# Moving two input tiles to the crossbar, five weight slices to a second DMA queue, and a gate vector to five rows, at the head of a TensorE-bound kernel

## The chip, the cores and the metric

One core of one Trainium2 chip. The metric is the device time of one execution in microseconds (us); each kernel is run several times and the median is given.

## The reference

Linear attention (A) and a token-mixing MLP (B) over the same 2048 x 640 input, mixed by a sigmoid gate. Cut to what matters here:

```python
x = A_x                                           # [1, 2048, 640] bf16
g = sigmoid((x * gate_w).sum(-1, keepdims=True))  # gate_w: [640]
qkv = x @ wqkv                                    # q, k, v; 32 heads of 20
pq, pk = phi(q), phi(k)
num = pq @ einsum(pk, v);  den = pq . sum(pk)     # linear attention
a = (num / den) @ wo
b = x1 + gelu(ln(x1) @ w3) @ w4                   # x1 = x + mix(gelu(ln(x) @ w1)) @ w2
out = g * a + (1 - g) * b
```

## The kernel before

TensorE needs x transposed (`xT`) as its stationary operand, the one that is loaded as weights. The 16 tiles of 128 tokens get it in two ways: tiles 0 to 3 are turned on TensorE (five 128 x 128 transposes a tile, then a copy out of PSUM, the memory that TensorE writes), tiles 4 to 15 by the crossbar, a transposing DMA from `x_tok` to `xT`. `wq` and `wk` (here `wkg`, with columns for the row sum and the gate) come in five slices of 160 KB, one for each 128 rows of the contraction. All big loads go through SyncE's queue, in this order:

```python
sch.dma("act", junk[:, 0, 0:32]..., "touch")               # a few bytes of wqkv, ScalarE's queue
dma_in(x_tok[:, 0:2, :], ..., "x01")                       # tiles 0 and 1, 320 KB
dma_in(x_tok[:, 2:4, :], ..., "x23")
for k in range(KD):                                        # KD = 5
    load_wq(k)
for k in range(KD):
    dma_in(wkg[:, k, 0:D], A_wqkv[128 * k:128 * (k + 1), D:2 * D], "wk%d" % k)
dma_in(wkg[:, :, D + 2:D + 3], gate_w.rearrange("(k p o) -> p k o", p=128, o=1), "gw", noncontig=True)
for c in range(1, NCH):                                    # tiles 4 to 15, four at a time
    dma_in(x_tok[:, 4 * c:4 * c + 4, :], ..., "xc%d" % c)  # 640 KB
    for t in range(4 * c, 4 * c + 4):
        sch.dma("sp", xT[:, :, 128 * t:128 * (t + 1)], x_tok[:, t, :], ..., transpose=True)
```

The head of TensorE's program. `stream` takes several tiles through one weight slice before it goes to the next, so a slice is needed later; each (tile, slice) is a pair of matmuls, 512 and 128 columns wide:

```python
addA(("warm",), 0.0, lambda: warmup(NWARM, 427.0))         # NWARM = 5
for i in range(4):
    addA(("tx", i), 0.28, lambda i=i: t_x(i))              # turn tile i on TensorE
    if i % 2:
        addA(("warm", i), 0.0, lambda: warmup(NWARM2, 300.0))  # NWARM2 = 2
addA(("q", 3), 5.44, q_four)                               # q of tiles 0..3, slice by slice
addA(("k", 0), 1.36, k_first)
for i in range(1, 4):
    addA(("k", i), 1.36, lambda t=i: k_tile(t))
for i in range(4, NT + 2):
    ...                                                    # q and k of tile i, and so on
```

Waits are derived from the tiles that each operation reads and writes. (The rest of the kernel, which the change does not touch, is cut.)

Of the kernel before, what the change touches and what calls it, by code (L numbers as in the profile page):

```python
# [5 lines left out]
BF16 = mybir.dt.bfloat16  # L6
F32 = mybir.dt.float32
ACTF = mybir.ActivationFunctionType
# [3 lines left out]
D = 640  # L12
# [3 lines left out]
NT = S // 128  # L16
# [408 lines left out]
def _build(nc, A_x, A_wqkv, A_wo, B_w1, B_w2, B_w3, B_w4, gate_w, out, dbg=None, stop=None):  # L425
# [45 lines left out]
    def psb(b, n0, n1):  # L471
        return ps[:, b, :].bitcast(BF16)[:, n0:n1]

    ones_c = pa.alloc("ones_c", [128, 768], BF16)
    ident = pa.alloc("ident", [128, 128], BF16)
    mask = pa.alloc("mask120", [128, 6, 20], BF16)
    mask_t = pa.alloc("mask_t", [128, 6, 20], BF16)
    negh = pa.alloc("negh", [128, 4], F32)
    st1 = pa.alloc("st1", [128, 8, NT], F32)
# [57 lines left out]
    def pair():  # L537
        best = None
        for k_ in range(4):
            q_ = (bank_rr[0] // 2 + k_) % 4  # L540
            tf = 0.0
            ok = True
            for b in (2 * q_, 2 * q_ + 1):
                if b in bank_pend or b in bank_hold:
                    ok = False
                lk = sch.locks.get(b)
                if lk is not None:
                    tf = max(tf, sch.ev_time.get((lk[1].sem, lk[1].val), 1e18))
            if ok and (best is None or tf < best[0]):
                best = (tf, 2 * q_)  # L550
        b = best[1]
        bank_rr[0] = b + 2
        bank_pend.update((b, b + 1))
        return b
# [94 lines left out]
    def activation(out_ap, in_ap, func, scale=1.0, bias=0.0, accum=None):  # L649
        rd = [in_ap] + [a for a in (scale, bias) if not isinstance(a, (int, float))]  # L650
        wr = [out_ap] + ([accum] if accum is not None else [])
        n = nfree(out_ap)
        cost = max(150.0, 100.0 + 0.833 * n + (70.0 if in_psum(in_ap) else 0.0)) + 45.0 * (len(rd) - 1)
        if accum is not None:
            cost += 91.0
        st_ = ACT_SET.get(func)
        if st_ is not None and st_ != sch.act_func:
            cost += 1290.0
            sch.act_func = st_
        if accum is not None:  # L660
            return act(lambda e: e.activation(out_ap, in_ap, func, bias=bias, scale=scale, accum_out=accum), rd, wr, cost=cost)  # L661
        return act(lambda e: e.activation(out_ap, in_ap, func, bias=bias, scale=scale), rd, wr, cost=cost)  # L662

    def memset(engf, ap, val):
        return engf(lambda e: e.memset(ap, val), [], [ap])  # L665

    def copy(engf, out_ap, in_ap):
        cost = None
        if engf is dve and in_ap.dtype == BF16 and out_ap.dtype == BF16:
            cost = 65.0 + nfree(out_ap) / 1.92  # L670
        return engf(lambda e: e.tensor_copy(out_ap, in_ap), [in_ap], [out_ap], cost=cost)
# [7 lines left out]
    def dma_in(out_ap, in_ap, key, **kw):  # L679
        return sch.dma("sp", out_ap, in_ap, key, **kw)  # L680

    sch.dma("act", junk[:, 0, 0:32].rearrange("p (k f) -> p k f", k=2),
            A_wqkv.rearrange("(k p) f -> p k f", p=128)[:, 0:KD:KD - 1, 0:16], "touch")
    dma_in(x_tok[:, 0:2, :], x2[0:256, :].rearrange("(n p) d -> p n d", p=128), "x01")
    def load_wq(k):
        dma_in(wq[:, k, :], A_wqkv[128 * k:128 * (k + 1), 0:D], "wq%d" % k)

    dma_in(x_tok[:, 2:4, :], x2[256:512, :].rearrange("(n p) d -> p n d", p=128), "x23")
    for k in range(KD):
        load_wq(k)  # L690
    for k in range(KD):
        dma_in(wkg[:, k, 0:D], A_wqkv[128 * k:128 * (k + 1), D:2 * D], "wk%d" % k)
    dma_in(wkg[:, :, D + 2:D + 3], gate_w.rearrange("(k p o) -> p k o", p=128, o=1), "gw", noncontig=True)
    for c in range(1, NCH):
        dma_in(x_tok[:, 4 * c:4 * c + 4, :], x2[512 * c:512 * (c + 1), :].rearrange("(n p) d -> p n d", p=128), "xc%d" % c)
        for t in range(4 * c, 4 * c + 4):
            sch.dma("sp", xT[:, :, 128 * t:128 * (t + 1)], x_tok[:, t, :], "trx%d" % (t % 4), transpose=True)

    k_done = {}

# [18 lines left out]
            n = min(R6, D - R6 * r)  # L719
            sch.dma("pool", wo_aug[0:n, r, :], A_wo[R6 * r:R6 * r + n, :], "wo", group_total=6, deps=dp)  # L720

    memset(pool, ones_c[:], 1.0)
    aselect(ident[:], ones_c[:, 0:128], [[-1, 128]], ALU.is_equal, 0, 1)
    memset(pool, wkg[:, :, D:D + 2], 1.0)
    memset(pool, negh[:], -0.5)
# [14 lines left out]

    IT = _Items()
    NWARM = 5
    NWARM2 = 2

    def t_x(t):
        b = bank()
        tr_group(b, [x_tok[:, t, 128 * k:128 * (k + 1)] for k in range(KD)])
        src = psb(b, 0, D).rearrange("p (k c) -> p k c", k=KD)
        dst = xT[:, :, 128 * t:128 * (t + 1)]
        if t % 2:  # L750
            activation(dst, src, ACTF.Copy)
        else:
            copy(dve, dst, src)

    def phi(b, dst, after_exp=None):
        se = slot("E", 3)
        src = psf[:, 512 * b:512 * b + D]
        activation(Er[:, se, :], src, ACTF.Exp)
        if after_exp is not None:
            after_exp()  # L760
        ts(dve, Er[:, se, :], Er[:, se, :], 1.0, EPS_PHI, ALU.min, ALU.add)
        return stt(dst, src, 1.0 + EPS_PHI, Er[:, se, :], ALU.add, ALU.max)

    def k_tile(t):
        tok = slice(128 * t, 128 * (t + 1))
        b = pair()
        mm_group(ps[:, b, 0:512], [(xT[:, k, tok], wkg[:, k, 0:512]) for k in range(KD)])
        mm_group(ps[:, b + 1, 0:131], [(xT[:, k, tok], wkg[:, k, 512:D + 3]) for k in range(KD)])
        k_out(t, b)
# [57 lines left out]
    def warmup(n, cyc):  # L827
        b = bank()

        def fn(e):  # L830
            ins = None
            for _ in range(n):
                ins = e.matmul(ps[:, b, :], ones_c[:, 0:128], ones_c[:, 128:640], start=True, stop=True)  # L833
            return ins
        pe(fn, [ones_c[:, 0:640]], [ps[:, b, :]], cost=n * cyc)
# [5 lines left out]
        mm_group(ps[:, b + 1, 0:128], [(xT[:, k, tok], wq[:, k, 512:D]) for k in range(KD)])  # L841
        phi(b, pq_tok[:, t, :])

    def stream(tiles, w, n2, land, done):
        nxt = {t: 0 for t in tiles}
        bs = {t: pair() for t in tiles}
        now = 0.0
        while nxt:
            t = next((t for t in tiles if t in nxt and nxt[t] * land <= now), min(nxt, key=lambda t: nxt[t]))
            now = max(now, nxt[t] * land) + 0.272  # L850
            k, b = nxt[t], bs[t]
            l = xT[:, k, 128 * t:128 * (t + 1)]

            def fn(e, l=l, b=b, k=k):
                e.matmul(ps[:, b, 0:512], l, w[:, k, 0:512], start=(k == 0), stop=(k == KD - 1))  # L855
                return e.matmul(ps[:, b + 1, 0:n2], l, w[:, k, 512:512 + n2], start=(k == 0), stop=(k == KD - 1))  # L856
            pe(fn, [w[:, k, 0:512 + n2], l], [ps[:, b, 0:512], ps[:, b + 1, 0:n2]], cost=272.0)
            nxt[t] += 1
            if nxt[t] == KD:
                del nxt[t]  # L860
                done(t, b)

    def q_four():
        stream(range(4), wq, 128, 0.5, lambda t, b: phi(b, pq_tok[:, t, :]))

    def k_out(t, b):
        k_done[t] = phi(b, pk_tok[:, t, :], lambda: activation(lr[:, t, :], ps[:, b + 1, 129:131], ACTF.Copy))
        activation(junk[:, 0, :], x_tok[:, t, :], ACTF.Square, accum=st1[:, 1, t:t + 1])

    def k_first():  # L870
        stream(range(1), wkg, 131, 0.0, k_out)

    def addA(name, dur, fn, deps=()):
        IT.add("A", name, dur, fn, deps)

    addA(("warm",), 0.0, lambda: warmup(NWARM, 427.0))
    for i in range(4):
        addA(("tx", i), 0.28, lambda i=i: t_x(i))
        if i % 2:
            addA(("warm", i), 0.0, lambda: warmup(NWARM2, 300.0))  # L880
    addA(("q", 3), 5.44, q_four)
    addA(("k", 0), 1.36, k_first)
    for i in range(1, 4):
        addA(("k", i), 1.36, lambda t=i: k_tile(t))
    for i in range(4, NT + 2):
        if i < NT:
            addA(("q", i), 1.36, lambda t=i: q_tile(t))
            addA(("k", i), 1.36, lambda t=i: k_tile(t))
        for t in range(3) if i == 4 else (i - 2,):
            addA(("g0", t), 0.27, lambda t=t: gt_step(0, t, t + 1), deps=[(("k", t), 2.0)])  # L890

    IT.add("LW", ("lw1",), 0.0, load_w1, deps=[(("k", 5), 0.0)])
    IT.add("LW", ("lw2",), 0.0, load_w2, deps=[(("k", 8), 0.0)])
# [276 lines left out]
            IT.add("W3", ("w3", c, j), 1.08, lambda c=c, j=j: w3_group(c, j), deps)  # L1170
        IT.add("W3", ("w3h", c), 0.76, lambda c=c: w3_half(c))
    for t in range(NT):
        deps = [(("zb",), 1.0), (("q", max(t, 3)), 2.0)]
        if t < 7:
            i = (5 * t) // 2 + 3
            deps.append((("w1", i // KD, i % KD), 0.0))
        else:
            i = 2 * (t - 7)
            deps.append((("w3", i // KFF, i % KFF), 0.0))
        IT.add("QN", ("qs", t), 0.0, lambda t=t: qn_sum(t), deps)  # L1180
        IT.add("QN", ("qn", t), 0.0, lambda t=t: qn_scale(t), [(("qs", t), 0.0)])
        IT.add("QT", ("qt", t), 0.0, lambda t=t: qt_tile(t), deps=[(("qn", t), 3.2), (("w2", NT - 1), 0.5), (("t2", NT - 1), 0.0)])
# [60 lines left out]
```

## Time and profile before

| | before |
|---|---|
| median of 3 runs known at first | 266.19 us |
| span of the profiled run | 264.6 us |
| TensorE (PE) busy | 260.2 us, 98% |
| first q matmul | 6.71 us |
| first wk matmul (the first 20 pairs are done) | 12.14 us |

The page's first line, its line of busy times, and the first line of its part on the chain of work that ended last:

```profile
span 264.6 us, 4340 instructions
PE 260.2 (98%) x1729; PEld 136.7 (52%) x1729; DVE 145.8 (55%) x242; ACT 107.9 (41%) x218; POOL 91.4 (35%) x148
...
PE 98%; DVE 0%; POOL 0%; issue 0%; POOLq 0%
```

TensorE is the whole chain. A microsecond that TensorE idles is a microsecond of the result. The list of TensorE's waits (who waited for what, total us, times, longest) has one line, at the start:

```profile
PE ps L833 <- POOL ones_c L665: 1.6, 1, 1.6
```

The head, from the timeline of TensorE (start, duration, engine, line, operation, out<-in, count). A busy time overlaps the next one a little, as matmuls are pipelined; read the starts.

```profile
1.59 2.32 PE L833 MATMUL ps<-ones_c 128*128 128x512 bf16 x5 [1.59 <-POOL ones_c L665]
3.91 1.25 PE L617 MATMUL ps<-ident,x_tok 128*128 128x128 bf16 x10
4.95 0.94 PE L833 MATMUL ps<-ones_c 128*128 128x512 bf16 x2
5.72 0.72 PE L617 MATMUL ps<-ident,x_tok 128*128 128x128 bf16 x10
6.28 0.60 PE L833 MATMUL ps<-ones_c 128*128 128x512 bf16 x2
6.71 0.38 PE L855 MATMUL ps<-wq,xT 128*128 128x512 bf16 x1
```

SyncE's queue over the same stretch (start and duration of the issue, not of the transfer):

```profile
1.81 2.36 SPq L283 DMA_DIRECT2D wq<-in_A_wqkv_dram  x5
4.21 2.33 SPq L283 DMA_DIRECT2D wkg<-in_A_wqkv_dram  x5
6.58 0.43 SPq L282 DMA_DIRECT2D wkg<-in_gate_w_dram  x1
7.06 0.54 SPq L283 DMA_DIRECT2D x_tok<-in_A_x_dram  x1
12.94 6.17 SPq L279 DMA_TRANSPOSE xT<-x_tok  x4
```

And the view of the tile `wkg`, its line on the time from issue to landing (the largest is that of gate_w):

```profile
DMA to landing us min/median/max: 3.6/3.7/4.8
```

### The profile page before, as it was taken

How to read it: one execution, taken by the hardware profiler on the slowest of the kernel's cores; microseconds unless marked ns; L12 is line 12 of the kernel's file. 1: busy time of each engine (PE TensorE's matmuls, PEld its weight loads, DVE VectorE, ACT ScalarE, POOL GpSimd, SP SyncE). 2: the span in 40 equal slices, each digit the busy share in tenths (PEclk: the TensorE clock that was granted, in tenths of full speed). 3: DMA queues.
4: the chain of work that ended last, by engine and by line, in shares of the span. 5: the costliest groups of instructions: out<-in, count | busy, mean ns of one | idle time of the engine just before them, and what ended most of it. 6: DMA issues, size and time to landing. Idle time of an engine off the chain costs nothing.

```text
span 264.6 us, 4340 instructions
## 1 busy us (share of the span) xinstructions
PE 260.2 (98%) x1729; PEld 136.7 (52%) x1729; DVE 145.8 (55%) x242; ACT 107.9 (41%) x218; POOL 91.4 (35%) x148
## 2 busy tenths in 40 slices
PE   7999999999999999999999999999999999999995
PEld 4555555555555555554445445545454455445553
DVE  1486877899713797999776986321212121122242
ACT  3496677741365757766651211212321322121000
POOL 4003995759764025688730204000120011021020
PEclk9999999999999999999999999999999999999999
DMA  7765998634567897255456831120000200002011
GB/s 229 218 100 133 199 182 136 191 85 22 102 122 106 252 379 137 39 99 49 92 113 126 111 63 25 42 85 2 0 0 11 90 0 0 2 0 102 0 50 50
DMA packets 50627, 24.78 MB, mean 94 GB/s; under 512 B 42028, under 2 KB 49197, under 8 KB 50608
## 3 DMA queue, kind: packets, MB, share of 16 engines
q1 hardware_dynamic: 49184, 21.23, 37.0%
q0 software_dynamic: 1152, 3.28, 5.4%
q8 instruction: 13, 0.21, 0.4%
q14 instruction: 6, 0.05, 0.1%
q10 hardware_dynamic: 272, 0.01, 0.1%
HBM read 12.05 MB, written 2.62 MB: 55 GB/s over the span
## 4 chain that ended last, share of the span: by engine, by line
PE 98%; DVE 0%; POOL 0%; issue 0%; POOLq 0%
PE ps L606 61%; PE ps L1102 21%; PE ps L785 8%; PE ps L855 2%; PE ps L833 1%; PE ps L1084 1%; PE ps L1024 1%; PE ps L617 1%; PE ps L941 1%; PE ps L856 1%; DVE x_tok L645 0%; POOL ones_c L665 0%; POOLq L1228 0%
## 5 line engine op out<-in xcount | busy, mean ns | idle before, releaser
L662 ACT ACTIVATE h2T<-ps 128x512 bf16<-128x512 f32 x52 | 31.0, 596 | 83.8 <-PE ps L606 83.7
L606 PE MATMUL ps<-xnT,w_58 128*128 128x512 bf16 x260 | 60.9, 379 | 0.0
L1102 PE MATMUL ps<-w_84,h2T 128*128 128x512 bf16 (+1 forms) x416 | 58.8, 299 | 0.0
L628 POOL TENSOR_SCALAR abx<-x_tok,stg 128x640 f32<-128x640 bf16 x16 | 13.9, 873 | 107.6 <-DVE x_tok L645 71.2
L1102 PEld LDWEIGHTS ps<-w_84,h2T 128*128 128x128 bf16 x416 | 32.7, 98 | 27.8 <-issue 1.3
L645 DVE SCALAR_TENSOR_TENSOR x_tok<-ps,stg,abx 128x640 bf16<-128x640 f32 (+2 forms) x17 | 14.3, 845 | 51.7 <-PE ps L1102 51.7
L606 PEld LDWEIGHTS ps<-xnT,w_58 128*128 128x128 bf16 x260 | 24.0, 98 | 24.8 <-issue 1.0
L645 DVE SCALAR_TENSOR_TENSOR abx<-ps,stg,abx 128x640 f32<-128x640 f32 x16 | 14.1, 882 | 27.9 <-PE ps L606 24.9
L662 ACT ACTIVATE Er<-ps 128x640 bf16<-128x640 f32 x32 | 22.4, 704 | 13.7 <-PE ps L606 8.8
L662 ACT ACTIVATE hsT<-ps 128x512 bf16<-128x512 f32 (+1 forms) x32 | 18.9, 593 | 14.6 <-PE ps L606 14.3
L661 ACT ACTIVATE junk<-x_tok 128x640 bf16<-128x640 bf16 x32 | 23.6, 736 | 2.0 <-DVE x_tok L643 1.7
L606 PE MATMUL ps<-M_sb,pqnT 128*128 128x512 bf16 (+1 forms) x160 | 24.0, 299 | 0.0
L606 PE MATMUL ps<-xnT,w_59 128*128 128x512 bf16 x100 | 23.9, 379 | 0.0
L785 PE MATMUL ps<-pk_tok,x_tok 128*128 128x512 bf16 (+1 forms) x160 | 23.9, 299 | 0.0
L606 PE MATMUL ps<-w_60,hsT 128*128 128x512 bf16 (+1 forms) x160 | 23.7, 299 | 0.0
L606 PE MATMUL ps<-wkg,xT 128*128 128x512 bf16 (+1 forms) x150 | 22.6, 300 | 0.0
L628 POOL TENSOR_SCALAR xn<-x_tok,st_54 128x640 bf16<-128x640 bf16 x16 | 17.3, 1087 | 7.1 <-DMA xnT<-xn 7.0
L606 PEld LDWEIGHTS ps<-w_60,hsT 128*128 128x128 bf16 x160 | 13.2, 98 | 12.2
L606 PEld LDWEIGHTS ps<-M_sb,pqnT 128*128 128x128 bf16 x160 | 13.1, 98 | 12.2 <-issue 0.6
L628 POOL TENSOR_SCALAR xn<-x_tok,st_55 128x640 bf16<-128x640 bf16 x16 | 16.7, 1052 | 5.1 <-DMA xnT<-xn 4.7
L606 PE MATMUL ps<-wq,xT 128*128 128x512 bf16 (+1 forms) x120 | 18.3, 299 | 0.0
L628 DVE TENSOR_SCALAR Er<-Er 128x640 bf16<-128x640 bf16 x32 | 12.0, 376 | 10.2 <-ACT Er L662 10.0
(74 smaller groups left out, 264.5 us busy)
## 6 DMA issues: line engine op xcount, KB each, us to landing
w_58<-in_B_w_dram SPq DMA_DIRECT2D x1, 2160.0 KB, 8.6
w_84<-in_B_w_dram SPq DMA_DIRECT2D x1, 2080.0 KB, 14.2
x_tok<-in_A_x_dram SPq DMA_DIRECT2D x3, 640.0 KB, 5.9
out_dram<-x_tok SPq DMA_DIRECT2D x3, 640.0 KB, 3.5
wq<-in_A_wqkv_dram SPq DMA_DIRECT2D x5, 160.0 KB, 3.8
wkg<-in_A_wqkv_dram SPq DMA_DIRECT2D x5, 160.0 KB, 3.7
wv<-in_A_wqkv_dram POOLq DMA_DIRECT2D x1, 800.0 KB, 6.0
wo_aug<-in_A_wo_dram POOLq DMA_DIRECT2D x5, 150.0 KB, 4.9
```

Of the source, the lines that this page charges most:

```text
L606: ins = e.matmul(out_ap, l, r, start=(i == 0), stop=(i == n - 1))
L617: ins = e.transpose(o, s_, ident[:])
L628: return engf(lambda e: e.tensor_scalar(out_ap, in_ap, s1, s2, op0, op1), rd, [out_ap], cost=cost)
L645: return dve(lambda e: e.scalar_tensor_tensor(out_ap, in0, scalar, in1, op0, op1), rd, [out_ap], cost=cost)
L661: return act(lambda e: e.activation(out_ap, in_ap, func, bias=bias, scale=scale, accum_out=accum), rd, wr, cost=cost)
L662: return act(lambda e: e.activation(out_ap, in_ap, func, bias=bias, scale=scale), rd, wr, cost=cost)
L785: ins = e.matmul(o, l, r, start=(t0 + q_ == 0), stop=(t0 + q_ == NT - 1))
L833: ins = e.matmul(ps[:, b, :], ones_c[:, 0:128], ones_c[:, 128:640], start=True, stop=True)
L855: e.matmul(ps[:, b, 0:512], l, w[:, k, 0:512], start=(k == 0), stop=(k == KD - 1))
L856: return e.matmul(ps[:, b + 1, 0:n2], l, w[:, k, 512:512 + n2], start=(k == 0), stop=(k == KD - 1))
L941: ins = e.matmul(o, l, r_, start=st_, stop=sp_, skip_group_check=True)
L1102: ins = e.matmul(o, l, r, start=False, stop=(i == KFF - 1))
```

## The change

Its intent: TensorE turns two tiles fewer, so dense work starts sooner. Tiles 2 and 3 go to the crossbar, to be ready behind k of tiles 0 and 1. wk goes over ScalarE's queue, held until the first slice of wq has landed, so that it does not crowd wq out. gate_w is loaded as 5 rows of 128 and turned on TensorE, in place of a gather of single elements.

The core of the diff (cut: allocation of `gw_t`, the rewritten `stream`, the lags of later items, an earlier memset of `ones_c`, and the copies of turned tiles, which are now all VectorE's):

```diff
-    sch.dma("act", junk[:, 0, 0:32].rearrange("p (k f) -> p k f", k=2), A_wqkv...[:, 0:KD:KD - 1, 0:16], "touch")
+    sch.dma("act", junk[0:16, 0, 0:80].rearrange("p (k f) -> p k f", k=KD),
+            A_wqkv[:, 0:16].rearrange("(k e r) f -> e r k f", k=KD, r=8)[:, 0, :, :], "touch")
+    sch.dma("act", gw_t[0:KD, :], gate_w.rearrange("(k p) -> k p", p=128), "gw")
     # x01, x23, then wq[0..4] on SyncE's queue, as before
+    activation(negh[:, 0:1], ones_c[:, 0:1], ACTF.Exp)          # a dummy, loads the table
     for k in range(KD):
-        dma_in(wkg[:, k, 0:D], A_wqkv[...], "wk%d" % k)
-    dma_in(wkg[:, :, D + 2:D + 3], gate_w.rearrange("(k p o) -> p k o", p=128, o=1), "gw", noncontig=True)
+        sch.dma("act", wkg[:, k, 0:D], A_wqkv[...], "wk%d" % k, deps=wq_ev[0:1])
+    cross_xT(2)
+    cross_xT(3)
     ...
-    NWARM2 = 2
+    NWARM2 = 4
     addA(("warm",), 0.0, lambda: warmup(NWARM, 427.0))
-    for i in range(4):
+    for i in range(2):
         addA(("tx", i), 0.28, lambda i=i: t_x(i))
-        if i % 2:
-            addA(("warm", i), 0.0, lambda: warmup(NWARM2, 300.0))
-    addA(("q", 3), 5.44, q_four)
-    addA(("k", 0), 1.36, k_first)
-    for i in range(1, 4): ...
+    addA(("warm2",), 0.0, lambda: warmup(NWARM2, 300.0))
+    addA(("gate",), 0.05, gate_col)      # turn gw_t, copy into wkg's gate column (VectorE)
+    addA(("q", 1), 2.72, q_two)          # q of tiles 0 and 1, slice by slice
+    addA(("k", 1), 2.72, k_two)          # k of tiles 0 and 1, slice by slice
+    for i in range(2, NT + 2): ...       # q and k of tile i
```

More of the change, by code (lines that the diff above doesn't have):

```diff
@@ L476, in _build @@
     mask = pa.alloc("mask120", [128, 6, 20], BF16)
+    gw_t = pa.alloc("gw_t", [128, 128], BF16)
     mask_t = pa.alloc("mask_t", [128, 6, 20], BF16)
@@ L680, in dma_in, with load_wq, cross_xT, load_xc @@
         return sch.dma("sp", out_ap, in_ap, key, **kw)
-    sch.dma("act", junk[:, 0, 0:32].rearrange("p (k f) -> p k f", k=2),
-            A_wqkv.rearrange("(k p) f -> p k f", p=128)[:, 0:KD:KD - 1, 0:16], "touch")
+    sch.dma("act", junk[0:16, 0, 0:80].rearrange("p (k f) -> p k f", k=KD),
+            A_wqkv[:, 0:16].rearrange("(k e r) f -> e r k f", k=KD, r=8)[:, 0, :, :], "touch")
+    sch.dma("act", gw_t[0:KD, :], gate_w.rearrange("(k p) -> k p", p=128), "gw")
+    def load_wq(k):
+        return dma_in(wq[:, k, :], A_wqkv[128 * k:128 * (k + 1), 0:D], "wq%d" % k)
+    def cross_xT(t):
+        sch.dma("sp", xT[:, :, 128 * t:128 * (t + 1)], x_tok[:, t, :], "trx%d" % (t % 4), transpose=True)
+    def load_xc(c):
+        dma_in(x_tok[:, 4 * c:4 * c + 4, :], x2[512 * c:512 * (c + 1), :].rearrange("(n p) d -> p n d", p=128), "xc%d" % c)
     dma_in(x_tok[:, 0:2, :], x2[0:256, :].rearrange("(n p) d -> p n d", p=128), "x01")
-    def load_wq(k):
-        dma_in(wq[:, k, :], A_wqkv[128 * k:128 * (k + 1), 0:D], "wq%d" % k)
     dma_in(x_tok[:, 2:4, :], x2[256:512, :].rearrange("(n p) d -> p n d", p=128), "x23")
+    wq_ev = [load_wq(k) for k in range(KD)]
+    memset(pool, ones_c[:], 1.0)
+    activation(negh[:, 0:1], ones_c[:, 0:1], ACTF.Exp)
     for k in range(KD):
-        load_wq(k)
-    for k in range(KD):
-        dma_in(wkg[:, k, 0:D], A_wqkv[128 * k:128 * (k + 1), D:2 * D], "wk%d" % k)
-    dma_in(wkg[:, :, D + 2:D + 3], gate_w.rearrange("(k p o) -> p k o", p=128, o=1), "gw", noncontig=True)
+        sch.dma("act", wkg[:, k, 0:D], A_wqkv[128 * k:128 * (k + 1), D:2 * D], "wk%d" % k, deps=wq_ev[0:1])
+    cross_xT(2)
+    cross_xT(3)
     for c in range(1, NCH):
-        dma_in(x_tok[:, 4 * c:4 * c + 4, :], x2[512 * c:512 * (c + 1), :].rearrange("(n p) d -> p n d", p=128), "xc%d" % c)
+        load_xc(c)
         for t in range(4 * c, 4 * c + 4):
-            sch.dma("sp", xT[:, :, 128 * t:128 * (t + 1)], x_tok[:, t, :], "trx%d" % (t % 4), transpose=True)
+            cross_xT(t)
     k_done = {}
@@ L720, in load_wvo @@
             sch.dma("pool", wo_aug[0:n, r, :], A_wo[R6 * r:R6 * r + n, :], "wo", group_total=6, deps=dp)
-    memset(pool, ones_c[:], 1.0)
     aselect(ident[:], ones_c[:, 0:128], [[-1, 128]], ALU.is_equal, 0, 1)
@@ L749, in t_x, with gate_col @@
         dst = xT[:, :, 128 * t:128 * (t + 1)]
-        if t % 2:
-            activation(dst, src, ACTF.Copy)
-        else:
-            copy(dve, dst, src)
+        copy(dve, dst, src)
+    def gate_col():
+        b = bank()
+        o = psb(b, 0, KD)
+        pe(lambda e: e.transpose(o, gw_t[0:KD, :], ident[0:KD, 0:KD]), [gw_t[0:KD, :], ident[:]], [o], cost=64.0)
+        copy(dve, wkg[:, :, D + 2:D + 3], o.rearrange("p (k o) -> p k o", o=1))
     def phi(b, dst, after_exp=None):
@@ L842, in q_tile, with stream @@
         phi(b, pq_tok[:, t, :])
-    def stream(tiles, w, n2, land, done):
-        nxt = {t: 0 for t in tiles}
-        bs = {t: pair() for t in tiles}
-        now = 0.0
-        while nxt:
-            t = next((t for t in tiles if t in nxt and nxt[t] * land <= now), min(nxt, key=lambda t: nxt[t]))
-            now = max(now, nxt[t] * land) + 0.272
-            k, b = nxt[t], bs[t]
+    def stream(order, w, n2, done):
+        bs = {}
+        for t, k in order:
+            if k == 0:
+                bs[t] = pair()
+            b = bs[t]
             l = xT[:, k, 128 * t:128 * (t + 1)]
@@ L857, in stream, with q_two @@
             pe(fn, [w[:, k, 0:512 + n2], l], [ps[:, b, 0:512], ps[:, b + 1, 0:n2]], cost=272.0)
-            nxt[t] += 1
-            if nxt[t] == KD:
-                del nxt[t]
+            if k == KD - 1:
                 done(t, b)
-    def q_four():
-        stream(range(4), wq, 128, 0.5, lambda t, b: phi(b, pq_tok[:, t, :]))
+    def q_two():
+        stream([(t, k) for k in range(KD) for t in range(2)], wq, 128, lambda t, b: phi(b, pq_tok[:, t, :]))
     def k_out(t, b):
@@ L868, in k_out, with k_two @@
         activation(junk[:, 0, :], x_tok[:, t, :], ACTF.Square, accum=st1[:, 1, t:t + 1])
-    def k_first():
-        stream(range(1), wkg, 131, 0.0, k_out)
+    def k_two():
+        stream([(t, k) for k in range(KD) for t in range(2)], wkg, 131, k_out)
     def addA(name, dur, fn, deps=()):
@@ L876, in _build @@
     addA(("warm",), 0.0, lambda: warmup(NWARM, 427.0))
-    for i in range(4):
+    for i in range(2):
         addA(("tx", i), 0.28, lambda i=i: t_x(i))
-        if i % 2:
-            addA(("warm", i), 0.0, lambda: warmup(NWARM2, 300.0))
-    addA(("q", 3), 5.44, q_four)
-    addA(("k", 0), 1.36, k_first)
-    for i in range(1, 4):
-        addA(("k", i), 1.36, lambda t=i: k_tile(t))
-    for i in range(4, NT + 2):
+    addA(("warm2",), 0.0, lambda: warmup(NWARM2, 300.0))
+    addA(("gate",), 0.05, gate_col)
+    addA(("q", 1), 2.72, q_two)
+    addA(("k", 1), 2.72, k_two)
+    for i in range(2, NT + 2):
         if i < NT:
@@ L888, in _build @@
             addA(("k", i), 1.36, lambda t=i: k_tile(t))
+        if i < 4:
+            continue
         for t in range(3) if i == 4 else (i - 2,):
-            addA(("g0", t), 0.27, lambda t=t: gt_step(0, t, t + 1), deps=[(("k", t), 2.0)])
+            addA(("g0", t), 0.27, lambda t=t: gt_step(0, t, t + 1), deps=[(("k", max(t, 1)), 2.0)])
     IT.add("LW", ("lw1",), 0.0, load_w1, deps=[(("k", 5), 0.0)])
@@ L1172, in _build @@
     for t in range(NT):
-        deps = [(("zb",), 1.0), (("q", max(t, 3)), 2.0)]
+        deps = [(("zb",), 1.0), (("q", max(t, 1)), 2.0)]
         if t < 7:
```

## The prediction

> **What bounds it.** TensorE, nearly without a gap. The page gives PE 260.2 us busy of a 264.6 us span (98%), and the chain of waits is PE for 98%. The list of waits shows PE waiting once: 1.6 us at the start, for the memset of ones_c. So a change pays only by removing PE work or by starting the dense work sooner.
>
> **The head, from the timeline.** Warm-up matmuls run from 1.59 us, weight loads 0.43 us apart; x tiles 0 and 1 are turned from 3.91 to 4.95, two more warm-ups run to 5.72, tiles 2 and 3 to 6.28, two warm-ups to 6.71, and then q matmuls run densely, 0.27 us per 512+128 pair. The Trainium skill, "TensorE: Matmul & The Clock Gate" (section "Wait — 56ns, not 53.3ns?"), gives 426.7 ns cold and 215.7 ns warm for N = 512; the trace agrees (0.43 us early, 0.27 us for 512 plus 128 later).
>
> **Removed.** Ten transposes on PE (5.72 to 6.28, 0.56 us), two ScalarE evictions of 0.70 us (off the chain), and the gate_w gather, which took 4.8 us to land and sat before the next 640 KB of x: issued at 7.06, that released the crossbar only at 12.94. **Added:** one 5-row transpose, about 0.06 us of PE; a tiny DVE copy; two crossbar transposes, 1.2 to 1.3 us of SP issue each, 3.4 us to landing. The dummy Exp changes little: the table load already ran at 1.30. **Moved:** wk issues go to ScalarE's queue and wait for wq0. Warm-ups stay four.
>
> **Critical path.** Dense q should start at 4.95 + 0.77 + 0.43 + 0.06 = about 6.2 us instead of 6.7. That is the whole gain, 0.5 us; the remaining matmuls are the same.
>
> **What can eat it.** The stream now runs 0.54 us per k slice over two tiles, where four gave 1.09. wq0 should land near 5.5 us (issue 1.81 plus 3.7); the slices stay 0.6 to 0.9 us ahead of need. wk issues then run from 5.5 to about 8 us and, sharing engines with the two transposes and x of tiles 4 to 7, land (my estimate) at 8.5 to 11.3; k needs them from 8.9 to 11.1. The skill's "DMA: Bandwidth & Descriptors" ("Issuing engines are not separate DMA queues") says that transfers started by different engines share the same 16 engines, so a second queue buys no bandwidth; the trace shows 320 to 365 GB/s from 3 to 8 us, already full. I expect 0 to 0.5 us of stall on the last wk slices. Tiles 2 and 3 are needed at 11.7 and 14.4, and should be there by about 10. Tiles 4 to 7 are needed from 17.1; before, the first came near 16.3, and without the gather it should come sooner.
>
> **Predicted time.** 265.8 us, 8 in 10 within 264.9 to 266.7 (before: 266.19). Faster by over 2%: 0.01; within 2%: 0.98; slower by over 2%: 0.01.
>
> **What would show it.** Start: the first wq matmul at 6.0 to 6.4 us. Gather: crossbar of tile 4 issued by 12 us. wk: the first wkg matmul near 8.9, and no PE gap before 17 us; a gap between 8.9 and 11.6 with wkg as releaser is the stall feared. Then the k matmuls of tile 3 end near 17.1 against 17.6, and later landmarks are 0.5 us earlier. PE busy falls by about 0.5 us.
>
> **What would make it wrong.** wk or the transposes landing a microsecond late (no gain, or a loss up to 1 us); x01 landing at another time; the clock warming later; the order of work further down, planned from modelled times, coming out differently and moving 0.5 us either way.

## The result

The change made the kernel slower: 269.39 us median of six runs (268.86 to 269.85) against 266.56 us (266.0 to 267.31, six runs). The ratio is 1.0103 (95% interval 1.0080 to 1.0126). Ratios here are the mean time of one kernel's fast runs over that of the other's in the same rounds, so they are not quite the ratios of the medians.

The lines of the page after that answer to those above, and TensorE's waits:

```profile
span 267.1 us, 4325 instructions
PE 260.2 (97%) x1720; PEld 135.9 (51%) x1720; DVE 145.8 (55%) x243; ACT 106.6 (40%) x217; POOL 91.9 (34%) x148
...
PE 93%; DMA 4%; ACTq 1%; DVE 0%; SPq 0%; issue 0%
```

```profile
PE ps L865 <- DMA wkg<-in_A_wqkv_dram: 2.3, 3, 1.0
PE ps L845 <- POOL ones_c L666: 1.6, 1, 1.6
PE ps L618 <- DMA x_tok<-in_A_x_dram: 0.2, 1, 0.2
```

The chain no longer stays on TensorE from the start: it runs from SyncE's issues through the landing of the first wq slice, ScalarE's issues of wk (they wait for that slice) and the landing of the last wk slice. Its two long pieces in the head, from the view of the chain (start, duration):

```profile
1.83 3.63 DMA wq<-in_A_wqkv_dram
...
7.73 6.35 DMA wkg<-in_A_wqkv_dram
```

The timeline of TensorE shows where it waited:

```profile
4.15 1.25 PE L618 MATMUL ps<-ident,x_tok 128*128 128x128 bf16 x10 [0.24 <-DMA x_tok<-in_A_x_dram]
5.19 1.21 PE L845 MATMUL ps<-ones_c 128*128 128x512 bf16 x4
...
6.44 0.39 PE L865 MATMUL ps<-wq,xT 128*128 128x512 bf16 x1
...
9.16 0.38 PE L865 MATMUL ps<-wkg,xT 128*128 128x512 bf16 x1
...
10.26 0.39 PE L865 MATMUL ps<-wkg,xT 128*128 128x512 bf16 x1 [0.39 <-DMA wkg<-in_A_wqkv_dram]
...
12.03 0.39 PE L865 MATMUL ps<-wkg,xT 128*128 128x512 bf16 x1 [1.04 <-DMA wkg<-in_A_wqkv_dram]
...
14.13 0.39 PE L865 MATMUL ps<-wkg,xT 128*128 128x512 bf16 x1 [0.83 <-DMA wkg<-in_A_wqkv_dram]
...
14.69 1.52 PE L607 MATMUL ps<-wq,xT 128*128 128x512 bf16 x10
```

q started 0.27 us sooner than before and k followed without a break at 9.16. Then TensorE waited three times, for slices 1, 2 and 4 of wk. The first 20 pairs (q and k of two tiles) were done at 14.69 us; before, its first 20 pairs (q of four tiles) were done at 12.14. That is 2.55 us, and the span grew by 2.5 us: what lies behind the head takes as long as before and is only shifted. The sum closes if one reads starts. At the three stops the next pair starts 0.82, 1.48 and 1.26 us after the one before it (from 9.44, 10.55 and 12.87 in the same timeline) where 0.27 is usual. That is 2.75 us lost, of which the view calls 2.3 waiting and counts the rest as busy; less the 0.27 us by which q began sooner, it is the 2.5.

The issues of wk on ScalarE's queue, and those of SyncE's queue (two fences, two answers):

```profile
5.48 2.94 ACTq L283 DMA_DIRECT2D wkg<-in_A_wqkv_dram  x5
```

```profile
1.83 2.36 SPq L283 DMA_DIRECT2D wq<-in_A_wqkv_dram  x5
5.02 2.61 SPq L279 DMA_TRANSPOSE xT<-x_tok  x2
7.67 0.60 SPq L283 DMA_DIRECT2D x_tok<-in_A_x_dram  x1
14.72 5.44 SPq L279 DMA_TRANSPOSE xT<-x_tok  x4
```

The view of the tile `wkg` (the median landing grew from 3.7 to 5.4 us), and the DMA view for 7 to 11 us, with one line for each queue (q10 is ScalarE's, q1 SyncE's; packets, MB, share of the 16 engines):

```profile
DMA to landing us min/median/max: 3.6/5.4/6.3
```

```profile
q10 hardware_dynamic: 499, 0.57, 75.9%
q1 hardware_dynamic: 1110, 0.29, 36.1%
```

So the engines are occupied nearly throughout (the shares add up to 112% of the 16 engines' time, so the times of packets overlap), and yet in these four microseconds only 0.57 MB of wk and 0.29 MB of everything else moved, 216 GB/s. Most of that 0.29 MB is the two crossbar transposes. From the completion events in the trace, the times (us) at which the slices of wk had fully landed:

| | wk0 | wk1 | wk2 | wk3 | wk4 |
|---|---|---|---|---|---|
| before | 7.96 | 8.39 | 8.86 | 9.28 | 9.99 |
| after | 9.10 | 10.22 | 11.98 | 12.47 | 14.08 |

Before, 640 KB of wk took 2.0 us from the first to the last landing; after, 5.0 us.

### The profile page after: what moved, and what is told of

Same layout as the page of the kernel before. It is cut to its first block, busy times and chain, and to the rows that moved or that the text cites. A ratio compares the mean times of both kernels' runs of the same rounds, so it can differ in the third digit from the quotient of the medians.

```text
span 267.1 us, 4325 instructions
## 1 busy us (share of the span) xinstructions
PE 260.2 (97%) x1720; PEld 135.9 (51%) x1720; DVE 145.8 (55%) x243; ACT 106.6 (40%) x217; POOL 91.9 (34%) x148
## 4 chain that ended last, share of the span: by engine, by line
PE 93%; DMA 4%; ACTq 1%; DVE 0%; SPq 0%; issue 0%
PE ps L607 61%; PE ps L1110 21%; PE ps L797 8%; DMA wkg<-in_A_wqkv_dram 2%; DMA wq<-in_A_wqkv_dram 1%; PE ps L1092 1%; PE ps L1032 1%; ACTq L283 1%; PE ps L949 1%; DVE x_tok L646 0%; SPq L283 0%; PE ps L865 0%; PE ps L866 0%
## 5 line engine op out<-in xcount | busy, mean ns | idle before, releaser
L646 DVE SCALAR_TENSOR_TENSOR abx<-ps,stg,abx 128x640 f32<-128x640 f32 x16 | 14.1, 882 | 27.9 <-PE ps L607 24.9
L663 ACT ACTIVATE hsT<-ps 128x512 bf16<-128x512 f32 (+1 forms) x32 | 18.9, 593 | 14.6 <-PE ps L607 14.3
L607 PE MATMUL ps<-wkg,xT 128*128 128x131 bf16 (+1 forms) x140 | 21.4, 300 | 0.0
L607 PE MATMUL ps<-wq,xT 128*128 128x128 bf16 (+1 forms) x140 | 21.3, 299 | 0.0
L607 PEld LDWEIGHTS ps<-w_61,hsT 128*128 128x128 bf16 x160 | 13.2, 98 | 12.2
L607 PEld LDWEIGHTS ps<-M_sb,pqnT 128*128 128x128 bf16 x160 | 13.1, 98 | 12.2 <-issue 0.6
```

Source lines behind the costliest of these rows:

```text
L607: ins = e.matmul(out_ap, l, r, start=(i == 0), stop=(i == n - 1))
L646: return dve(lambda e: e.scalar_tensor_tensor(out_ap, in0, scalar, in1, op0, op1), rd, [out_ap], cost=cost)
L663: return act(lambda e: e.activation(out_ap, in_ap, func, bias=bias, scale=scale), rd, wr, cost=cost)
```

## The experiments

Three accounts were open. **Crossbar**: the two transposing DMAs move beside wk and occupy the engines for longer than their bytes suggest. **Late issue**: the gate on wq0 and ScalarE's queue start wk 1.3 to 1.6 us later (5.48 against 4.21 for the first, 7.73 against 6.11 for the last), and that alone is too late. **Sharing**: x of tiles 4 to 7 (640 KB, issued at 7.67) takes half of the bandwidth while wk moves.

All outputs are right. "20 pairs" is the time at which TensorE had done its first 20 q and k pairs, read from the timeline as for 14.69 above (in e7, which keeps the order of the kernel before, as for its 12.14); wk4 is the landing of the last wk slice from the trace.

| kernel | first q | wk4 landed | 20 pairs done | span of the profile | median (runs) | ratio to before |
|---|---|---|---|---|---|---|
| before | 6.71 | 9.99 | 12.14 | 264.6 | 266.56 (6) | |
| the change | 6.44 | 14.08 | 14.69 | 267.1 | 269.39 (6) | 1.0103 |
| e1_wk_sp | 7.16 | 9.89 | 13.05 | 265.5 | 266.69 (4) | 0.9997 |
| e2_ungated | 6.93 | 10.08 | 13.24 | 265.7 | 267.70 (4) | 1.0031 |
| e3_no_cross_x1_late | 7.34 | 10.93 | 12.82 | 267.6 | 267.42 (4) | 1.0009 |
| e4_x1_late | 6.97 | 13.45 | 14.34 | 267.8 | 268.71 (4) | 1.0075 |
| e5_no_cross | 8.05 | 12.90 | 13.77 | 266.2 | 268.10 (4) | 1.0053 |
| e6_plain_copies | 7.83 | 13.51 | 14.28 | 266.7 | 269.69 (4) | 1.0106 |
| e7_gate_only | 7.58 | 10.44 | 13.02 | 265.5 | 267.30 (4) | 1.0017 |
| e8_head | 5.47 | 10.89 | 15.81 | 268.3 | 270.21 (5) | 1.0129 |
| e9_plain_x1_late | 6.94 | 11.10 | 12.41 | 269.3 | one look | |
| e10_wk_sp_warm1 | 5.67 | 9.72 | 11.20 | 264.0 | 266.36 (6) | 0.9977 |
| e11_one_cross_x1_late | 7.44 | 11.06 | 12.92 | 265.8 | one look | |
| e12_warm1 | 5.95 | 14.20 | 14.80 | 267.2 | 268.98 (4) | 1.0092 |

Two things help to read the table. First, where x is not held back (e1, e2, e5, e6, e7, e8, e12), the span differs from that before by what the "20 pairs" column differs, to 0.1 us: the head decides. (In e10 it differs by 0.3 us more; see there.) Second, the first q matmul depends on when TensorE's clock comes up. In e1, with the same instructions ahead of q as the change, warm-ups ran at 0.43 us each to the end and q began at 7.16, in the change at 6.44. The Trainium skill ("TensorE: Matmul & The Clock Gate", "What's actually happening") says that the activity window is free-running, so the moment varies by 500 ns either way; here the same instructions gave 6.44, 6.93, 6.97 and 7.16 us (the change, e2, e4, e1), which agrees. Runs of the kernel before lay between 265.85 and 267.88 us over all sessions; whether the same thing spreads them was not looked at.

### e1: wk back on SyncE's queue

```diff
-        sch.dma("act", wkg[:, k, 0:D], A_wqkv[...], "wk%d" % k, deps=wq_ev[0:1])
+        dma_in(wkg[:, k, 0:D], A_wqkv[...], "wk%d" % k)
```

Expected:

> Undoes the queue part alone: the five wk loads go back to SyncE's queue, after wq, ungated, and the two crossbar transposes of tiles 2 and 3 are issued behind them. All theories (crossbar beside wk; late gated issue; sharing with x of tiles 4 to 7) expect the same here: wk lands by about 10 us as in the kernel before, TensorE waits for no wk slice (2.3 us in the changed kernel), the first q matmul stays near 6.4 us, time 266.0 to 267.0. What may go wrong: x of tiles 4 to 7 is issued near 9.2 us, so tile 4 may come up to 1 us late (needed at about 17.3).

Measured: 266.69 us, ratio 0.9997 (0.9972 to 1.0023). wk4 landed at 9.89 us and the waits for wk are gone:

```profile
PE ps L845 <- POOL ones_c L666: 1.6, 1, 1.6
PE ps L618 <- DMA x_tok<-in_A_x_dram: 0.3, 1, 0.3
```

So the loss came from how wk travels, as far as these runs resolve (the interval is about 0.7 us either way). The transposes still took place, behind wk on the same queue, and TensorE waited for no slice. (First q was at 7.16, not near 6.4, because of the clock.) Nor does the 0.5 us that was forecast as gain show here, where no wait eats it (266.69 against 266.64 us for the kernel before). This run does not say which of gate, queue and transposes was at fault.

### e2: no gate

```diff
-        sch.dma("act", wkg[:, k, 0:D], A_wqkv[...], "wk%d" % k, deps=wq_ev[0:1])
+        sch.dma("act", wkg[:, k, 0:D], A_wqkv[...], "wk%d" % k)
```

Expected:

> Takes away the gate on wq0 alone; wk stays on ScalarE's queue and is issued from about 3.4 us, two microseconds sooner. Theory crossbar: the last slices still move beside the transposes, so some wait stays (0.5 to 1.5 us), time about 267 to 268. Theory late issue: the wait is gone, time 266.0 to 266.8. In both, wq now shares the engines with wk and its last slice may come late, up to 0.5 us of wait on wq.

Measured: 267.70 us, ratio 1.0031 (1.0009 to 1.0054). Both accounts missed in part. No wait for wk was left, against the crossbar account as I had written it: issued from 1.93 us, wk shared the engines with wq and had landed by 10.08, before the transposes landed (10.55 and 11.12); by the packet records its packets started from 4.0 to 9.4 us and those of the transposes only from 8.7 on. The time did not go down to 266.8 either: the same sharing delayed wq, whose last slice landed at 9.89 us (7.55 in the change). TensorE and its weight loads waited for it:

```profile
PEld ps L865 <- DMA wq<-in_A_wqkv_dram: 1.3, 3, 0.6
PE ps L865 <- DMA wq<-in_A_wqkv_dram: 0.2, 1, 0.2
```

So the gate is part of the cause, as it pushes wk into the same stretch as the transposes; and what it was meant to protect (wq) did need protection.

### e3 and e4: with and without the transposes, x of tiles 4 to 7 held back

Both hold the 640 KB of x back until wk4 has landed, so that sharing with x is out of the picture. e4 keeps the transposes, e3 turns tiles 2 and 3 on TensorE.

```diff
 # both
-        load_xc(c)
+        load_xc(c, wk_ev[-1:] if c == 1 else ())
 # e3 alone
-    cross_xT(2)
-    cross_xT(3)
+    for i in (2, 3):
+        addA(("tx", i), 0.28, lambda i=i: t_x(i))    # ahead of the gate column and q
```

Expected of e3:

> Takes the crossbar transposes of tiles 2 and 3 away from wk (those tiles are turned on TensorE before q, as in the kernel before, 0.6 us more PE) and holds x of tiles 4 to 7 back until wk4 has landed, so that wk moves alone; it is still gated on wq0 and issued by ScalarE. Theory crossbar: wk4 lands by 10.5 us, TensorE waits for no slice, time 266.6 to 267.2. Theory late issue (gate and ScalarE's queue): wk4 lands at 12 us or later and TensorE still waits 1 us or more, time 268 or more.

Expected of e4:

> Keeps the two crossbar transposes beside wk and only holds back x of tiles 4 to 7 until wk4 has landed. Theory crossbar: the waits for wk1 and wk2 stay as they are (0.4 and 1.0 us), only that for wk4 (0.8 us) shrinks or goes; wk2 lands near 12 us; time 268 to 269. Theory sharing with x of tiles 4 to 7: all waits go, wk4 lands by 10.5 us, time about 266.3.

Measured: e3 landed wk4 at 10.93 us with no wait for wk, though wk was as late in its issue and on the same queue as in the change. Its waits:

```profile
PE ps L607 <- DMA xT<-x_tok: 2.2, 1, 2.2
PE ps L844 <- POOL ones_c L666: 1.6, 1, 1.6
PE ps L618 <- DMA x_tok<-in_A_x_dram: 0.3, 1, 0.3
```

Its q began 0.9 us later than the change's, but that does not hide a wait: with q at 6.44 the slices would be needed at about 9.16, 9.70, 10.25, 10.79 and 11.33 (my estimate, from the starts of the change and 0.54 us a slice), and they landed at 8.35, 8.79, 9.24, 10.55 and 10.93. Gate and ScalarE's queue alone do no harm. (Its time, 267.42 us from 266.33 to 269.33, is blurred by the hold itself: the profiled run waited 2.2 us for xT of tile 4.) e4 landed wk4 at 13.45 and waited 1.4 us for wk:

```profile
PE ps L866 <- DMA wkg<-in_A_wqkv_dram: 1.4, 3, 0.9
PE ps L607 <- DMA xT<-x_tok: 0.7, 2, 0.4
```

Its first q was 0.5 us later than the change's, which hides that much of the wait. The transposes cost 2.5 us of landing (13.45 against 10.93). x of tiles 4 to 7 costs wk4 0.6 us (13.45 against 14.08), which these single profiles hardly resolve: wk0 to wk3 landed 0.65 to 1.0 us *later* in e4 than in the change, though the edit only takes traffic away. That wk4 followed wk3 by 0.33 us in e4, and by 1.6 and 1.9 us in the change and e12, does point to x as what held wk4 there.

### e5 and e6: other traffic beside wk

e5 takes the two transposes out but leaves x of tiles 4 to 7 free; e6 puts two plain copies of the same 160 KB each, from the same tiles, in their place.

```diff
 # both: tiles 2 and 3 on TensorE, as in e3
-    cross_xT(2)
-    cross_xT(3)
 # e6 adds
+    for t in (2, 3):
+        sch.dma("sp", pq_tok[:, t + 12, :], x_tok[:, t, :], "cp%d" % t)
```

Expected of e5:

> Takes the two crossbar transposes away from wk (tiles 2 and 3 turned on TensorE ahead of q), but leaves x of tiles 4 to 7 free: it is issued near 4.2 us and shares the engines with wk; gate and ScalarE's queue stay. Theory crossbar: plain sharing costs little, wk4 lands near 11 to 11.7 us, needed near 12, waits for wk at most 0.3 us, time 266.6 to 267.2. Theory sharing: 640 KB of x beside 800 KB of wk is more traffic than the two transposes were, so wk4 lands at 13 us or later and TensorE waits 1 us or more.

Expected of e6:

> Puts two plain copies of the same 160 KB each, from the same x tiles within the on-chip memory, in the place of the two crossbar transposes (tiles 2 and 3 are turned on TensorE ahead of q, so results stay right). Theory crossbar: it is the transposing that holds the engines, plain copies of the same bytes let wk4 land by 11.7 us and TensorE waits under 0.4 us for wk; wk packets average under 80 ns (116 ns beside the transposes). Theory any traffic: as in the changed kernel, wk2 near 12 us, wk4 near 14 us, waits of 1.5 us or more.

Measured: e5 landed wk4 at 12.90 with 0.3 us of wait for wk; e6 at 13.51 with 0.6 us. Both landings were later than the crossbar account allowed (11.7 at most), and the landing in e5 is nearly what the sharing account said (13). The runs were not clean: without 2.6 us of transpose issue ahead of it on SyncE, x of tiles 4 to 7 was issued at 4.21 and 6.24 us instead of 7.67, so 640 KB moved beside wk and not behind it. What they do show is that in these two runs ordinary traffic delayed wk4 too, by 2.0 and 2.6 us against e3: taking the transposes away is no cure if x then moves beside wk. The waits were short because q began 1.4 to 1.6 us later than in the change. In time e6 lost as much as the change (1.0106 against 1.0103), with no transpose beside wk. One part of the crossbar account held: wk's 1280-byte packets averaged 59 ns in e5 and 61 in e6, under the 80 that it allowed, so here wk came late without its packets being held up. (e6's profile was its fastest run, 268.46 against a median of 269.69; what the slower ones waited for was not seen.)

### e9 and e11: the same bytes without transposing, and half the dose

Both hold x back, as e3 and e4 do. e9 has the two plain copies; e11 has one transpose (tile 2), with tile 3 turned on TensorE.

```diff
 # e9: e3 plus
+    for t in (2, 3):
+        sch.dma("sp", pq_tok[:, t + 12, :], x_tok[:, t, :], "cp%d" % t)
 # e11: e4, but
-    cross_xT(3)
+    addA(("tx", 3), 0.28, lambda: t_x(3))
```

Expected of e9:

> The run with plain copies did not isolate the transposes, as x of tiles 4 to 7 was then issued 1.4 us sooner. Here the two plain copies stand beside wk and x is held until wk4 has landed, so this differs from the run with the crossbar and x held (wk4 at 13.4 us) and from the run with neither (10.9 us) in one thing. If a transpose costs the engines what its bytes cost: wk4 lands near 13.4 us here too. If it costs more than its bytes (my account now): 320 KB at about 330 GB/s add 1 us, wk4 lands at 11.6 to 12.2 us.

Expected of e11:

> Dose: one crossbar transpose (tile 2) beside wk in place of two, tile 3 turned on TensorE, x of tiles 4 to 7 held until wk4 has landed. With none wk4 landed at 10.9 us, with two at 13.4 us. If the transposes take the engines' time in proportion, wk4 lands near 12.2 us (11.8 to 12.6). If it is the number of queues that compete and not the transposes, it lands at 13 us or later, or at 11 us.

Measured: e9 landed wk4 at 11.10 us, e11 at 11.06. Of the loads in the head, these two runs, e3 and e4 differ only in what stands beside wk. The four in the DMA view from 7 to 11 us. First e4 (two transposes), then e9 (two plain copies), then e3 (nothing), then e11 (one transpose); columns as above, q10 is wk:

```profile
q10 hardware_dynamic: 387, 0.44, 70.6%
q1 hardware_dynamic: 1006, 0.25, 42.4%
```

```profile
q10 hardware_dynamic: 707, 0.80, 64.5%
q1 hardware_dynamic: 196, 0.21, 15.1%
```

```profile
q10 hardware_dynamic: 653, 0.74, 60.7%
q1 hardware_dynamic: 2, 0.00, 0.1%
```

```profile
q10 hardware_dynamic: 696, 0.79, 73.3%
q1 hardware_dynamic: 361, 0.08, 12.8%
```

The landings of all slices (us), from the completion events:

| beside wk | wk0 | wk1 | wk2 | wk3 | wk4 |
|---|---|---|---|---|---|
| nothing (e3) | 8.35 | 8.79 | 9.24 | 10.55 | 10.93 |
| two plain copies (e9) | 8.51 | 9.40 | 10.28 | 10.71 | 11.10 |
| one transpose (e11) | 9.44 | 9.90 | 10.31 | 10.67 | 11.06 |
| two transposes (e4) | 10.09 | 11.00 | 12.64 | 13.12 | 13.45 |

Beside two transposes wk moved 0.44 MB in four microseconds; beside two plain copies of the same bytes 0.80 MB, nearly all of it. wk occupied the engines as long for half of the data. From the packet records of the trace, a 1280-byte packet of wk took 116 ns on average in e4, 66 in e9, 68 in e3 and 76 in e11, with a median of 55 to 58 ns in all four: some packets are held up. Of wk's 640 packets, 88 took over 200 ns in e4, 14 in e9, 24 in e3 and 32 in e11. The transposes themselves come in 256-byte packets, 1280 for two tiles, that took 32.0 us of engine time in e4; the same bytes as plain copies took 14.6 in e9, in 256 packets of 1280 bytes. Spread over 16 engines (my estimate) that is 1.1 us more for the transposes' own packets, and the hold-ups of wk's packets (74.3 us of engine time against 42.2) are 2.0 us more: the larger part is what the neighbour suffers. So it is not the bytes that count. Whether it is the transposing itself, or that it comes in five times as many packets of a fifth of the size, these runs do not separate: no run put plain copies in 256-byte packets beside wk. My own range for e9 (11.6 to 12.2) missed too, on the low side. My dose reading missed by the number: one transpose should have landed wk4 near 12.2 us and landed it at 11.06. But wk4 is a poor yardstick there, as the table shows: one transpose delayed each of the first three slices by 1.1 us against e3 (two delayed them by 1.7, 2.2 and 3.4), and the difference goes only because wk3 came late in e3 by itself, 1.3 us after wk2. So one transpose does cost, and two cost more, how exactly these runs do not say. Against the plain copies the two transposes cost 2.4 us on wk2 and on wk4 alike. Each of these landings is from one profile (that beside two transposes was seen three times: 13.45 in e4, 14.08 in the change and 14.20 in e12, the last two with x free).

### e12: an earlier start for the changed kernel

```diff
-    NWARM2 = 4
+    NWARM2 = 1
```

Expected:

> The changed kernel with q started sooner: one warm-up matmul in place of four between the transposes and q, first q matmul near 5.7 us instead of 6.4. If the landing of the last wk slice sets the time (my account), nothing is gained: waits for wk grow by about 0.7 us in all, time 269.0 to 269.8 as for the changed kernel. If the time were set by the sum of TensorE's work and its start, it would fall by 0.7 us to about 268.7.

Measured: 268.98 us, ratio to before 1.0092 (1.0062 to 1.0122), against 1.0103 for the change: the intervals overlap. q started at 5.95 instead of 6.44, and the first 20 pairs were done at 14.80 instead of 14.69, because wk4 landed at 14.20. So the time came out as expected, but not in the way expected: the waits for wk did not grow by 0.7 us (2.2 against 2.3). The first three pairs of q ran 0.51, 0.53 and 0.39 us apart in place of 0.27, and the first wk pair came at 9.29 us against 9.16. The head start was gone before wk was needed, so this run does not test what a head start is worth. That it could not have helped follows from the last wait alone: the pairs of slice 4 cannot start before wk4 lands, in the change (14.13, landed 14.08) or here (14.24, landed 14.20).

### e7: the gate vector alone

The kernel before, with gate_w loaded as 5 rows and turned on TensorE, and nothing else of the change.

```diff
+    sch.dma("act", gw_t[0:KD, :], gate_w.rearrange("(k p) -> k p", p=128), "gw")
-    dma_in(wkg[:, :, D + 2:D + 3], gate_w.rearrange("(k p o) -> p k o", p=128, o=1), "gw", noncontig=True)
+    addA(("gate",), 0.05, gate_col)      # ahead of q_four
```

Expected:

> The kernel before with one part of the change alone: gate_w loaded as 5 rows over ScalarE's queue and turned on TensorE. All theories: x of tiles 4 to 7 lands 1 us or more sooner than 12.9 us, but TensorE never waited for it, so the time is that of the kernel before, 266.2 to 267.0, ratio 0.998 to 1.002. If x of tiles 0 and 1 lands at 4.1 us here (3.9 before), the small gate_w load is what delays it in the changed kernel; if 3.9, it is the new touch.

Measured: 267.30 us, ratio 1.0017 (0.9990 to 1.0043): no difference that these runs resolve. x of tiles 4 to 7 landed at 12.27 us, 0.65 us sooner than before (12.93) and not 1 us or more; its issue moved from 7.06 to 6.59. TensorE never waited for it. Tiles 0 and 1 landed at 4.00 us, between 3.86 (before) and the 4.10 to 4.18 of the kernels with the new touch, so it settles nothing about that quarter of a microsecond.

### e8 and e10: versions meant to beat both

e8 changed several things at once: e1, plus wq ahead of x of tiles 2 and 3, the old touch, gate_w loaded after the dummy Exp, one warm-up for four, and the gate column turned *after* q of tiles 0 and 1. e10 is e1 with one line changed.

```diff
 # e8, the line that mattered
-    addA(("gate",), 0.05, gate_col)
     addA(("q", 1), 2.72, q_two)
+    addA(("gate",), 0.05, gate_col)
 # e10: e1, but
-    NWARM2 = 4
+    NWARM2 = 1
```

Expected of e8:

> A version meant to beat both: the change with wk back on SyncE's queue ahead of the crossbar transposes, wq loaded ahead of x of tiles 2 and 3, the old touch, gate_w loaded after the dummy Exp and turned after q of tiles 0 and 1, and one warm-up matmul between the transposes and q where there were four, so that q matmuls themselves warm the clock. First q matmul near 5.6 us (6.7 before, 6.4 in the changed kernel), no waits on wq, wk or xT; time 265.4 to 266.1, ratio 0.995 to 0.998. If crossbar of tile 4 or 5 comes late (needed near 16.9 and 19.6 us), up to half of that is lost.

Expected of e10:

> wk back on SyncE's queue ahead of the crossbar, as in the first experiment, and one warm-up matmul between the transposes and q in place of four, so that q starts about 1 us sooner whatever the clock does. First q matmul near 5.7 us; wq slices may be waited for up to 0.3 us, crossbar of tiles 4 and 5 up to 0.5 us; time 265.5 to 266.4 against 266.6 to 266.9 for the kernel before, ratio 0.995 to 0.999.

Measured: e8 took 270.21 us (1.0129), the slowest of those that were timed more than once. q did start at 5.47, but then:

```profile
PE ps L865 <- DVE wkg L672: 2.9, 1, 2.9
```

The copy of the gate column stood behind the work on q's results in VectorE's program and came at 11.10 us, though the transpose that feeds it ran at 8.33. And after this stop the next pairs started 0.54 us apart until 14.8 us, at half the pace of the pairs before it (0.27), so the stop cost about 2 us beyond its 2.9. A mistake of mine in program order, of a kind worth knowing: on an engine that works in order, a tiny copy inherits the wait of what stands in front of it.

e10 took 266.36 us, ratio 0.9977 (0.9954 to 1.0000), inside what was expected. Its head is 0.94 us ahead of the kernel before at 20 pairs (11.20 against 12.14), of which 0.2 us went to a wait for xT of a later tile and the rest of the difference was not traced; the profiled span is 264.0 us against 264.6. It is the best of all the kernels here, clear of the changed kernel, and against the kernel before at the edge of what the runs resolve.

## Why the prediction was wrong

I predicted 265.8 us, within 264.9 to 266.7. Measured: 269.39.

- **TensorE is the chain, and only the head matters: right.** PE busy is 260.2 us before and after, and the span grew by the delay of the first 20 pairs (2.55 of 2.5 us). The 0.5 us by which PE busy should fall does not show (260.2 both times), as the three stops put as much back: they cost 2.75 us from start to start, and the view calls only 2.3 of it waiting.
- **First q at 6.0 to 6.4 us instead of 6.7: nearly right.** It was 6.44 where the sum gave 6.2, because tiles 0 and 1 landed at 4.10 instead of 3.86 us. There was luck in it as well: the same instructions began q at 6.93 to 7.16 us in e2, e4 and e1. This gain was then lost, as k waited for wk.
- **"wk issues then run from 5.5 to about 8 us": right** (5.48 to 8.42).
- **"land (my estimate) at 8.5 to 11.3 ... I expect 0 to 0.5 us of stall on the last wk slices": the step that failed.** The slices landed at 9.1 to 14.1 us, and TensorE waited 2.3 us for them, from within the stretch of the feared gap (8.9 to 11.6 us) to past it (14.13). The place was right (a stall of k on wk, from sharing engines with the transposes and x) and the term was mis-sized: 2.3 us of waiting, nearly five times the upper end of what I had allowed. I had counted the two transposes as 320 KB among others. With x held back, they delay the last wk slice by 2.5 us against nothing beside it and by 2.4 us against the same bytes copied plainly (e4 against e3 and e9), each from one profile. x of tiles 4 to 7 adds perhaps 0.6 us on wk4.
- **Why the gate matters: shown together, not alone.** Gate and ScalarE's queue without transposes leave TensorE no wait for wk (e3). No gate, with the transposes, leaves none for wk either, but some for wq (e2). wk on SyncE's queue ahead of the transposes leaves none at all (e1). So the loss needed both: wk held back until it moves at the same time as the transposes. (Other traffic in the place of the transposes can delay it too: x did in e5.) In e1 one queue's order kept them largely apart, in e2 the earlier issue did; whether the two would also hurt each other when interleaved in one queue was not tried. That queues on different engines share the same 16 DMA engines, as the prediction cited, agrees with the runs (two queues from 7 to 11 us, with shares that add up to 112% of 16 engines); what I left out was that an entry on the other queue can be dear.
- **"Tiles 2 and 3 ... should be there by about 10": half right.** They landed at 9.29 and 11.68 us, in time for TensorE, which was late itself.
- **"crossbar of tile 4 issued by 12 us": wrong.** It was issued at 14.72, as x of tiles 4 to 7 was now issued at 7.67 behind two transposes and took 7.0 us to land. Without the rest of the change the new gate load does bring it to 12.29 (e7), and no time is gained by that.

What stays open: how the cost grows from one transpose beside wk to two; by what mechanism single wk packets are held up, and whether small packets alone would do it; and which of the small loads delayed tiles 0 and 1 by 0.25 us.

## What to carry to other kernels

When a kernel waits only at its head, list for each slice of data when it is needed and when it lands, and count a transposing DMA not by its bytes but by the engine time that it takes and by the packets of its neighbours that it holds up. Here a load that had to arrive soon was safe on the same queue ahead of such transfers (e1), and not on another queue beside them; a gate that protects one load can push the next one into worse company. Once a landing sets the time, an earlier start of the compute engine cannot help, so check after each such change which of the two is last. And when a run hits the expected time, check that it did so in the expected way (e12 did not).

## What the Trainium skill lacked or had wrong

- "Advanced Engine Details and Errata", section "X-Bar Transpose (TRN2)", says that "TRN2 transpose DMAs are as fast as regular DMAs". (The next line of that section gives them about 90% of a plain copy's bandwidth.) In these runs the gap is wider: the packets of two transposes of 160 KB took 32.0 us of engine time, those of two plain copies of the same bytes 14.6, and the wk beside them landed its last slice at 13.45 and 11.10 us (e4, e9).
- "DMA: Bandwidth & Descriptors", "Queues, rings and completion order", says that each engine takes turns between the queues at the granularity of packets. The runs agree that both queues move at once (0.57 and 0.29 MB from 7 to 11 us), but no page says what a transposing queue costs its neighbour in time: wk packets averaged 116 ns beside two transposes and 66 beside plain copies (e4, e9), and hardly more than that beside one (76, e11).
- "DMA: Bandwidth & Descriptors", "Issuing engines are not separate DMA queues", says that a second issuing engine saves only issue time. It does not say that one can lose. Here, with the gate that the second queue also brought, wk4 landed at 14.08 us, and on one queue at 9.89 (the change, e1); on the second queue without the gate it landed at 10.08, but wq came late (e2).
